# An RWKV-6 scan with a mixture of adapters on one core: last gates selected on logits and applied transposed, last tile in halves, first r and k apart, three output sums on GpSimd, a new order

## The chip, the cores and the metric

The kernel runs on 1 core of a Trainium2 chip. The metric is the device time of one execution in microseconds (us). The profile shows one execution by the hardware profiler; "span" is the part of it that the instructions cover. The engines are PE (TensorE matmul), PEld (TensorE weight load), DVE (VectorE), ACT (ScalarE), POOL (GpSimd) and SP (SyncE, which here only issues DMAs); "SPq" and "POOLq" are the instruction queues of SP and POOL.

## What is computed

Four batches of 768 steps, 8 heads of 48 channels. A recurrent attention with a decaying state, and behind it a top-2 mixture of eight rank-16 adapters:

```python
# per step t:   y[t] = r[t] . (state + (u*k[t]) x v[t]);   state = w[t]*state + k[t] x v[t]
x = y.transpose(0, 2, 1, 3).reshape(3072, 384)
logits = x @ w_gate                          # 8 experts
topk = two largest logits;  w = softmax over those two
out = x + sum over the two of  w_e * ((x @ A[e]) @ B[e])       # A: 384x16, B: 16x384
```

## The kernel before

The 3072 rows are 24 tiles of 128 steps; six consecutive tiles (a chunk row of one batch) share a running state. All 24 tiles are unrolled. Each step of each tile is a small Python function, called as `name.tile`; the list `ORDER` names all calls, and the scheduler is told to keep it (`manual_schedule` for all five engines). So every engine, SP with its DMAs included, executes its own instructions in the order in which they stand in that list, and an instruction that waits holds all that stand behind it on the same engine. The position of a call against calls of other engines has no effect by itself.

For tile t the steps are: `load_w`, `load_rk`, `load_v` (transfers, mostly two or four tiles at once); `ln` (ACT, log of w); `cs`, `ci` (PE, running sums of the logs) and `grow`, `exps` (ACT, exponentials); `mult` (DVE L362, r and k times these); `tr` (PE transposes) and `trev` (their copy); `amm` (PE, scores) and `aev` (DVE L453, masked scores); `rkp` and `dv` (POOL L379, L396), `dgmm` and `dgev` (the bonus term with u); `yi`, `ya` (PE, the tile's output); `kv` and `sev` (state and its copy); `xev` (DVE L529, the 128x384 result `xs`); `xk`, `xkev` (transpose of `xs` and its copy).

The adapters run in batches of tiles, `BATCHES = (4, 4, 4, 4, 4, 2, 1, 1)`, named after their last tile (3, 7, 11, 15, 19, 21, 22, 23): `lgmm` (PE logits), `gate` (ACT exp), `gmax` (DVE, the eight largest), `gsel` (DVE, those at or above the second), `gden` (DVE L579 sum of the two and L580 reciprocal), `gmul` (two POOL products, L599 and L600), `zmm` (PE, x @ A), `zw` (DVE L614, times the gates), `zT` (PE transpose) and `zTev` (its copy). Then per tile `dmm` (PE, @ B; where ACT makes the output an identity matmul adds `xs` first), `oev` (the 128x384 output `res`, on DVE L651, on ACT L649, or for tiles 22 and 23 on DVE L646 with the division) and `store` (SP L655, one DMA of 192 KB). `res` has 16 buffers; PSUM tiles of `y`, `xk`, `z`, `zT` and `d` share a ring of three.

SP issues the loads of w, of the first tiles and all stores. Its last entries in the old list, in order: the stores of tiles 2, 3, 1, 0, 6, 7, 4, 5, 11, 8, 9, 10, 14, 13, 12, 15, 17, 18, 19, 16, 20, 22, 21, 23, with loads between the first ones.

Of the kernel before, what the change touches and what calls it, by code (L numbers as in the profile page):

```python
# [8 lines left out]
F32 = mybir.dt.float32  # L9
# [42 lines left out]
SYNC = True  # L52
YA = False
COL = False
TAG = {('d', 22): 'y', ('d', 23): 'a_ps'}
ENGINES = {'out': {0: 'A', 3: 'A', 8: 'A', 12: 'A', 13: 'A', 15: 'A', 16: 'A', 18: 'A', 20: 'A', 21: 'A', 17: 'A'},
    'k_id16': {0: 'A'}, 'trev': {0: 'D', 5: 'D', 9: 'D'}, 'xkev': {-3: 'D', -2: 'D'}, 'sev': {0: 'D'}, 'dgev': {1:
    'D', 5: 'D'}, 'cast_v': {1: 'D'}, 'cast_b': {0: 'D'}, 'zTev': {3: 'A', 7: 'A', 11: 'A', 15: 'A', 19: 'A', 21: 'A',
    22: 'A', 23: 'A'}}
# [15 lines left out]
xkev.3 mult.7 amm.5 grow.8 dgev.5 aev.5 lgmm.2 trev.6 lgmm.3 gate.3 ci.8 gmax.3 gsel.3 load_rk.12 gden.3 zmm.3 exps.8
sev.4 load_v.12 ya.4 cs.9 tr.7 rkp.7 load_b.0 dv.4 xev.4 gmul.3 load_w.10 kv.6 ln.10 grow.9 trev.7 zw.3 dv.5 amm.6
ci.9 dgmm.6 yi.5 xk.4 zT.3 exps.9 sev.6 cast_b.0 xkev.4 mult.8 cs.10 rkp.8 aev.6 mult.9 zTev.3 kv.7 ya.5 dgmm.7
grow.10 sev.7 dgev.7 tr.8 dmm.2 ci.10 trev.8 ya.6 load_w.12 amm.7 kv.8 xev.5 xk.5 exps.10 cs.11 tr.9 sev.8 xkev.5 yi.7
oev.2 lgmm.4 aev.7 yi.8 grow.11 ln.12 dv.6 dv.7 xev.6 ci.11 dgmm.8 store.2 rkp.9 mult.10 kv.9 exps.11 xk.6 ya.7
# [10 lines left out]
grow.18 oev.6 gmax.11 amm.15 lgmm.12 trev.16 ci.18 dgev.15 dv.14 xk.13 exps.18 xkev.13 aev.15 yi.14 tr.17 ya.14 cs.19  # L90
store.3 yi.15 amm.16 zmm.11 sev.15 gsel.11 grow.19 trev.17 xev.14 ci.19 mult.18 xk.14 ln.20 tr.18 dgmm.16 ya.15
gden.11 load_w.22 exps.19 cs.20 xkev.14 dgmm.17 gmul.11 dv.15 dgev.17 yi.16 aev.16 load_rk.22 grow.20 trev.18 ya.16
mult.19 zw.11 kv.16 amm.17 store.1 zT.11 xev.15 ci.20 xk.15 dv.16 load_v.20 sev.16 exps.20 tr.19 cs.21 aev.17 rkp.19
zTev.11 xkev.15 grow.21 xev.16 dmm.8 dmm.11 amm.18 oev.8 mult.20 oev.11 lgmm.15 xk.16 yi.17 lgmm.13 lgmm.14 trev.19
gate.15 ci.21 dmm.9 ya.17 store.0 store.6 aev.18 gmax.15 kv.18 dv.17 xkev.16 xev.17 exps.21 amm.19 gsel.15 rkp.20
ln.22 ya.18 gden.15 oev.9 dgmm.19 dgmm.18 xk.17 store.7 store.4 store.5 dgev.19 sev.18 cs.22 gmul.15 xkev.17 dv.18
tr.20 grow.22 aev.19 zmm.15 yi.19 trev.20 lgmm.17 ci.22 ya.19 dv.19 rkp.21 exps.22 kv.19 xev.18 zw.15 sev.19 amm.20
store.11 store.8 zT.15 xev.19 cs.23 zTev.15 mult.21 dmm.10 store.9 dmm.13 rkp.22 oev.13 aev.20 xk.18 xkev.18 dgmm.20
tr.21 trev.21 xk.19 lgmm.16 mult.22 dmm.14 dgmm.21 oev.10 kv.20 xkev.19 rkp.23 dgev.21 amm.21 dmm.12 dv.20 lgmm.18
lgmm.19 yi.20 oev.14 grow.23 sev.20 gate.19 store.10 store.14 oev.12 aev.21 ya.20 dmm.15 ci.23 tr.22 exps.23 trev.22  # L100
gmax.19 yi.21 xev.20 gden.19 ya.21 xk.20 kv.21 dv.21 amm.22 mult.23 tr.23 store.13 store.12 oev.15 xkev.20 sev.21
gsel.19 zmm.19 gmul.19 trev.23 xev.21 store.15 dgmm.23 dgmm.22 xk.21 dgev.23 aev.22 xkev.21 amm.23 kv.22 sev.22 zw.19
zT.19 dv.22 yi.22 ya.22 dv.23 zTev.19 aev.23 xev.22 lgmm.20 lgmm.21 dmm.17 yi.23 ya.23 gate.21 gmax.21 oev.17 store.17
xk.22 xev.23 dmm.18 xkev.22 gsel.21 oev.18 dmm.19 zmm.21 gden.21 kv.23 lgmm.22 store.18 oev.19 store.19 xk.23 gmul.21
# [609 lines left out]
```

## Time and profile before

| | us |
|---|---|
| median of 3 runs (lowest, highest) | 86.1 (86.06, 86.43) |
| the profiled execution's own time | 85.72 |
| its span | 84.0 |
| PE, DVE, ACT, POOL busy | 76.6, 74.2, 68.9, 55.9 |
| DMA | 18.12 MB, mean 216 GB/s |

A windows view gives the busy time of each engine in a stretch of the span, then the granted TensorE clock (1.00 is full), the busy share of the 16 DMA engines, and GB/s moved. A row of groups gives line, engine, operation, tiles and shapes, the count, busy us and mean ns. A timeline row gives start, duration and the instruction, with the idle time before it and what ended it.

### The profile page before, as it was taken

What the parts mean: (1) busy time and instruction counts of PE and PEld (TensorE: products, weight loads), DVE (VectorE), ACT (ScalarE), POOL (GpSimd) and SP (SyncE); (2) the same over time, 40 slices, a digit from 0 to 9 for tenths busy, and PEclk for the clock granted to TensorE, in tenths of its full rate; (3) what the DMA queues carried; (4) which work ended last, traced back from release to release, by engine and by line L of the source; (5) the groups of instructions that cost most, each with busy time, mean ns of one, the idle gap of its engine ahead of it and who ended that gap; (6) DMA issues with size and microseconds to landing.
All of it is one profiled execution on the core that took longest, in us unless ns stands there. A gap on an engine that the chain in (4) does not pass through costs nothing.

```text
span 84.0 us, 3311 instructions
## 1 busy us (share of the span) xinstructions
PE 76.6 (91%) x1322; PEld 58.4 (69%) x1322; DVE 74.2 (88%) x157; ACT 68.9 (82%) x167; POOL 55.9 (67%) x89
## 2 busy tenths in 40 slices
PE   4897699999999999999999999999999999999710
PEld 1244276688887878788888688888779788887300
DVE  5019989999999999999999999999999999999740
ACT  6376679799999999999899989879898789866800
POOL 6306999689988667778999876379759483362000
PEclk9999999999999999999999999999999999999985
DMA  1899999999999999989999886988986026304681
GB/s 20 280 335 362 391 374 265 289 252 287 270 225 211 214 216 240 297 274 249 177 192 149 145 190 128 377 303 108 126 202 228 14 96 255 125 12 145 233 316 59
DMA packets 8943, 18.12 MB, mean 216 GB/s; under 512 B 992, under 2 KB 5216, under 8 KB 8928
## 3 DMA queue, kind: packets, MB, share of 16 engines
q1 hardware_dynamic: 6480, 11.82, 40.7%
q0 software_dynamic: 2448, 6.10, 40.3%
q8 instruction: 10, 0.16, 0.8%
q14 instruction: 5, 0.04, 0.2%
HBM read 19.29 MB, written 4.72 MB: 286 GB/s over the span
## 4 chain that ended last, share of the span: by engine, by line
PE 72%; DVE 15%; DMA 5%; issue 2%; SPq 1%; ACT 1%; ACTq 0%; DVEq 0%
PE trp L404 11%; PE xk_ps L538 9%; PE a_ps L442 8%; DVE rk L362 6%; PE y_ps L524 6%; PE s_ps L475 5%; DMA rk_first<-in_rk_dram 5%; PE d_ps L640 5%; PE z_ps L607 4%; PE y_ps L498 4%; PE cs_ps L351 4%; PE cs_ps L334 4%; PE cs_ps L333 3%; DVE at L453 3%; PE d_ps L639 2%; PE s_ps L559 2%
## 5 line engine op out<-in xcount | busy, mean ns | idle before, releaser
L453 DVE TENSOR_TENSOR at<-a_ps,strict 128x1024 f16<-128x1024 f32 x24 | 29.1, 1214 | 0.3
L379 POOL TENSOR_TENSOR rkp<-rk 128x384 f16<-128x384 f16 x20 | 18.2, 912 | 5.2 <-DVE rk L362 2.7
L396 POOL TENSOR_TENSOR dv<-v,dg 128x384 f32<-128x384 f16 x22 | 18.2, 835 | 3.7 <-ACT dg L200 3.0
L404 PE MATMUL trp<-ident,rk 128*128 128x128 bf16 x192 | 14.7, 219 | 0.5 <-DVE rk L362 0.5
L206 ACT COPY rkT<-trp 128x512 f32<-128x512 f32 x21 | 12.6, 600 | 1.2 <-PE trp L404 1.2
L404 PEld LDWEIGHTS <-rk 128*128 128x128 bf16 x192 | 11.7, 98 | 2.7 <-DVE rk L362 1.5
L346 ACT ACTIVATE e<-cs_ps 128x384 bf16<-128x384 f32 x24 | 12.0, 501 | 1.6 <-PE cs_ps L334 1.6
L529 DVE TENSOR_TENSOR xs<-dv,y_ps 128x384 f16<-128x384 f32 x24 | 13.1, 544 | 0.3 <-PE y_ps L524 0.2
L356 ACT ACTIVATE e<-cs_ps 128x384 bf16<-128x384 f32 x23 | 11.4, 497 | 1.8 <-PE cs_ps L351 1.7
L206 ACT COPY xkT<-xk_ps 128x384 f32<-128x384 f32 (+1 forms) x25 | 11.5, 462 | 0.4 <-PE xk_ps L538 0.2
L362 DVE TENSOR_TENSOR rk<-rk,e 128x768 bf16<-128x768 f16 x20 | 11.1, 560 | 0.0
L200 ACT CAST S_sb<-s_ps 128x384 bf16<-128x384 f32 x19 | 9.4, 492 | 0.7 <-PE s_ps L475 0.3
L442 PE MATMUL a_ps<-rkT 48*128 48x128 bf16 x192 | 9.5, 219 | 0.1
L324 ACT ACTIVATE logw<-w_in 128x768 f16<-128x768 f32 x11 | 9.3, 847 | 0.0
L334 PE MATMUL cs_ps<-logw,strict 128*128 128x384 f16 x24 | 8.2, 340 | 0.4 <-ACT logw L326 0.4
L538 PE MATMUL xk_ps<-ident,rkp 128*128 128x128 f16 x72 | 8.0, 219 | 0.4 <-POOL rkp L379 0.4
L351 PE MATMUL cs_ps<-logw,ident 128*128 128x384 f16 x24 | 8.0, 333 | 0.2 <-ACT e L346 0.2
L524 PE MATMUL y_ps<-v,at 128*128 128x48 f16 x176 | 8.0, 183 | 0.0
L538 PE MATMUL xk_ps<-ident,xs 128*128 128x128 f16 x72 | 8.0, 219 | 0.0
L524 PEld LDWEIGHTS <-at 128*128 128x128 f16 x192 | 7.3, 96 | 0.9
L362 DVE TENSOR_TENSOR rk<-rk_first,e 128x768 bf16<-128x768 f32 (+1 forms) x5 | 4.5, 913 | 3.7 <-DMA rk_first<-in_rk_dram 3.7
L640 PE MATMUL d_ps<-Ball,zT 128*128 128x384 f16 x24 | 7.5, 325 | 0.2 <-ACT zT L206 0.2
(76 smaller groups left out, 160.4 us busy)
## 6 DMA issues: line engine op xcount, KB each, us to landing
out_dram<-res SPq DMA_DIRECT2D x24, 192.0 KB, 2.6
w_in<-in_w_dram SPq DMA_DIRECT2D x11, 384.0 KB, 6.6
rk<-in_rk_dram POOLq DMA_DIRECT2D x10, 384.0 KB, 8.2
rk_first<-in_rk_dram SPq DMA_DIRECT2D x4, 384.0 KB, 6.0
v<-in_v_dram POOLq DMA_DIRECT2D x4, 384.0 KB, 8.5
v<-in_v_dram POOLq DMA_DIRECT2D x3, 192.0 KB, 10.6
w_in<-in_w_dram SPq DMA_DIRECT2D x2, 192.0 KB, 2.5
v_first<-in_v_dram SPq DMA_DIRECT2D x2, 192.0 KB, 7.1
```

Source lines behind the costliest of these rows:

```text
L206: nc.scalar.copy(out=out.bitcast(F32), in_=in_.bitcast(F32))
L346: nc.scalar.activation(out=e2[:, 0], in_=cs_ps[:, 0:HD], func=ACT.Exp, **(dict(bias=CENTRE) if CB else {}))
L362: return nc.vector.tensor_mul(rk2[:, lo:hi].rearrange("s m p h d -> s (m p h) d")[:, :, 0:D], st[t]["rk"][:, lo:hi].rearrange("s m (h d) - ...
L379: return nc.gpsimd.tensor_mul(p_, st[t]["rk"][:, 0], st[t]["rk"][:, 1])
L396: return nc.gpsimd.tensor_mul(dv_, st[t]["v16"], st[t]["dg"].rearrange("p (h o) -> p h o", o=1).to_broadcast([L, H, D]))
L404: nc.tensor.transpose(trp[:, m, p, :], rk2[:, m, p, :, :].rearrange("s a b -> s (a b)"), ident)
L442: nc.tensor.matmul(a_ps[:, g, p, :], lhsT=rkT[base:base + D, 1, p, :], rhs=rkT[base:base + D, 0, p, :], start=True, stop=True)
L453: nc.vector.tensor_mul(at, st[t]["a_ps"].rearrange("s g p f -> s (g p) f"), strict.to_broadcast([128, H, 128]))
L524: nc.tensor.matmul(d["y_ps"][:, h, :], lhsT=d["at"][:, g * P + p, :], rhs=d["v16"][:, h, :], start=(c == 0 and h == 0), stop=(h == H - 1), ...
L529: nc.vector.tensor_add(xs, st[t]["dv"].rearrange("p a b -> p (a b)"), st[t]["y_ps"].rearrange("p a b -> p (a b)"))
L538: nc.tensor.transpose(xk_ps[:, 3 * q + j, :], src[:, j * 128:(j + 1) * 128], ident16)
L640: nc.tensor.matmul(d_ps, lhsT=st[t]["zT"], rhs=Ball, start=not by_pe, stop=True)
```

## The change

- **First tile.** Its r and k come in two DMAs of 192 KB (`load_rr.0`, `load_kk.0`) instead of one of 384 KB.
- **Batches 22 and 23** (`TG`). The two largest are taken on the logits themselves; `gsel` writes a 128x128 mask, which `zT` transposes; `zmm` now makes two products, the logits repeated 16 times (weights `w16x`, made once by POOL in `m_wx`) and x @ A, both transposed; `zge` (ACT) is the exp of the first, `zw` (DVE) their product, and `zTev` (DVE) mask times product.
- **Tile 23 in halves.** `aev`, `ya`, `xev`, `oev` and `store` are split in two each.
- **Batches 3 to 21** (`GADD`). The sum of the two largest moves from DVE to POOL (`gadd`).
- **Output sums.** For tiles 4, 6 and 9 ACT copies the product and POOL adds `xs` (`oadd`); tiles 8, 12, 14 to 18 and 20 keep the sum on PE with ACT's copy. As before, ACT copies 11 outputs and DVE makes the rest.
- **Engines.** The casts of v (tile 1) and of B move from DVE to ACT; one identity cast, two small `dgev` and one `xkev` move from ACT to DVE.
- **Order.** `ORDER` is new throughout. On SP the stores now come in the order 0 (among the loads of w), 2, 7, 11, 5, 4, 19, 17, 16, 12, 1, 13, 15, 14, 6, 18, 10, 8, 20, 3, 21, 9, 22, and the two halves of 23. On DVE the outputs of tiles 22 and 23 come before the last steps of batches 15, 19 and 21.

```diff
+TG = (22, 23)
+GADD = (3, 7, 11, 15, 19, 21)
+RSPLIT = (0,)
...
-ENGINES = {'out': {0: 'A', 3: 'A', 8: 'A', 12: 'A', 13: 'A', 15: 'A', 16: 'A', 18: 'A', 20: 'A', 21: 'A', 17: 'A'},
...
+ENGINES = {'out': {4: 'G', 6: 'G', 8: 'A', 9: 'G', 12: 'A', 15: 'A', 14: 'A', 16: 'A', 17: 'A', 18: 'A', 20: 'A'},
+    'trev': {1: 'D', 3: 'D', 4: 'D'}, 'xkev': {-2: 'D', -3: 'D', 3: 'D'}, 'dgev': {1: 'D', 3: 'D', 5: 'D', 23: 'D'},
+    'sev': {6: 'D'}, 'zTev': {3: 'A', 7: 'A', 11: 'A', 15: 'A', 19: 'A', 21: 'A'}}
...
+xkev.18 dgmm.21 ya.19 xev.19 trev.21 kv.20 grow.23 amm.21 ci.23 dgev.21 rkp.22 tr.22 yi.20 ya.20 dv.20 xk.19 rkp.23
...
+oev.10 xkev.20 oadd.10 oadd.9 yi.22 dgmm.23 dgev.23 trev.23 ya.22 amm.23 dv.22 kv.22 sev.22 dmm.8 lgmm.13 lgmm.19
+lgmm.12 lgmm.14 yi.23 lgmm.15 oev.8 aeva.23 aevb.23 yaa.23 yab.23 xev.22 xk.22 gate.15 dv.23 xeva.23 xkev.22 lgmm.18
+lgmm.17 lgmm.16 xevb.23 kv.23 xk.23 xkev.23 lgmm.22 gmax.15 gmax.22 zmm.22 gsel.22 gsel.15 lgmm.23 gate.22 gden.22
+gmax.23 zge.22 zmm.23 zw.22 gsel.23 zT.22 zge.23 gate.23 zTev.22 zw.23 zT.23 gden.23 zTev.23 dmm.22 yi.21 lgmm.20
+dmm.23 zmm.15 oev.22 ya.21 oeva.23 gate.19 dv.21 gadd.15 gden.15 oevb.23 gmul.15 zw.15 zT.15 xev.21 gmax.19 zTev.15
+xk.21 dmm.15 oev.15 gsel.19 zmm.19 dmm.12 xkev.21 oev.12 dmm.14 lgmm.21 oadd.12 gadd.19 gden.19 oev.14 gmul.19 zw.19
+zT.19 dmm.13 zTev.19 oev.13 dmm.17 gate.21 gmax.21 oev.17 dmm.18 dmm.16 dmm.19 oev.19 oev.18 gadd.21 gden.21 gsel.21
+store.4 oadd.19 oadd.15 gmul.21 oadd.17 oev.16 oadd.16 oadd.13 oadd.14 zmm.21 zw.21 zT.21 zTev.21 store.19 oadd.18
+store.17 store.16 store.12 store.1 store.13 store.15 store.14 store.6 store.18 store.10 dmm.21 dmm.20 oev.21 oev.20
+oadd.8 oadd.20 store.8 store.20 store.3 oadd.21 store.21 store.9 store.22 storea.23 storeb.23
...
+    def load_half(t, m):
+        nc.sync.dma_start(out=st[t]["rk"][:, m], in_=flat(rk, t, 1, 2 * HD)[:, 0, m * HD:(m + 1) * HD])
...
+    def m_wx(t):
+        nc.gpsimd.tensor_copy(w16x, w16[:, :, ER:ER + E].rearrange("p j (e o) -> p j e o", o=1)
+                              .to_broadcast([128, 3, E, R]))
...
+    def aevh(t, lo):
...
+    def xevh(t, lo):
...
     def gate(t):
...
+        if t in TG:
+            ge = wk.tile([L, 1, 2], F32, name="ge2", bufs=2)
+            nc.scalar.activation(out=ge, in_=st[t]["top"][:, :, 0:2], func=ACT.Exp)
...
+    def gadd(t):
+        t0, n = gate_at[t]
+        st[t]["gsum"] = wk.tile([L, GMAX, 1], F32, name="gsum")[:, 0:n, :]
+        nc.gpsimd.tensor_add(st[t]["gsum"], st[t]["gtop"][:, :, 0:1], st[t]["gtop"][:, :, 1:2])
...
+            nc.vector.tensor_tensor(
+                out=st[t]["sel"], in0=lg_ps[:, t % NSLOT, :].rearrange("p (e o) -> p e o", o=1).to_broadcast([L, E, R]),
+                in1=st[t]["top"][:, :, 1:2].to_broadcast([L, E, R]), op=ALU.is_ge)
...
+    def zge(t):
+        st[t]["geT"] = wk.tile([ER, 128], F32, name="geT", bufs=2)
+        nc.scalar.activation(out=st[t]["geT"], in_=st[t]["z_ps"][:, 0, :], func=ACT.Exp)
...
+            for i in range(2):
+                for j in range(3):
+                    lhsT = w16x[:, j].rearrange("p e r -> p (e r)") if i == 0 else w16[:, j, 0:ER]
+                    nc.tensor.matmul(z_ps[:, i, :], lhsT=lhsT, rhs=st[t]["xT"][:, j, :], start=(j == 0), stop=(j == 2))
...
+            nc.vector.tensor_mul(st[t]["zg"], st[t]["z_ps"][:, 1, :], st[t]["geT"])
...
+            nc.vector.tensor_mul(zT_[:, 0, :], st[t]["zT_ps"][:, 0, :], st[t]["zg"])
...
+    def oadd(t):
+        if engine("out", t, "D") == "G":
+            return nc.gpsimd.tensor_add(st[t]["res"], st[t]["res"], st[t]["xs"])
...
+    def oevh(t, i):
+        c = slice(i * HD // 2, (i + 1) * HD // 2)
...
+        nc.vector.scalar_tensor_tensor(out=st[t]["res"][:, c], in0=st[t]["d_ps"][:, c], scalar=st[t]["den"],
+                                       in1=st[t]["xs"][:, c], op0=ALU.mult, op1=ALU.add)
...
+    def storea(t):
+        nc.sync.dma_start(out=out[t * 128:(t + 1) * 128, 0:HD // 2], in_=st[t]["res"][:, 0:HD // 2])
...
+    def storeb(t):
+        nc.sync.dma_start(out=out[t * 128:(t + 1) * 128, HD // 2:], in_=st[t]["res"][:, HD // 2:])
```

An `oadd` of a tile that is not on GpSimd issues nothing.

More of the change, by code (lines that the diff above doesn't have):

```diff
@@ L75 @@
[L75 to L79, printed above, removed]
@@ L90 @@
[L90 to L94, printed above, removed]
@@ L95 @@
[L95 to L104, printed above, removed]
@@ L416, in amm @@
         st[t]["a_ps"] = a_ps
+        if YA:
+            if t % NC:
+                st[t]["y_ps"] = pp.tile([L, H, D], F32, name="y_ps", **slot("y", t))
+            rows = [[(D, carried, t, p, 0) for p in range(P if t % NC else 0)] + [(128, score, t, p, 0) for p in range(P)],
+                    [(D, carried, t - 1, p, 1) for p in range(P if t and (t - 1) % NC else 0)]
+                    + [(128, score, t, p, 1) for p in range(P)]]
+            sent = [0, 0]
+            while rows[0] or rows[1]:
+                g = 0 if rows[0] and (not rows[1] or sent[0] <= sent[1]) else 1
+                n, fn, *args = rows[g].pop(0)
+                fn(*args)
+                sent[g] += n
+            return
         if t in PACK:
@@ L663 @@
                 before = done
-            elif f in ("rkp", "dv") and before is not None and SYNC:
+            elif f in ("rkp", "dv", "oadd", "zs") and None not in (done, before) and SYNC:
                 tc.add_manual_dep(done.ins, before.ins.name, mybir.DependencyInfo(
```

176 lines of the change are left out of this document (137 added, 39 removed).

## The prediction

> **What bounds the kernel now.** I read the page's engine table first, then a windows view cut at two points: the start of the first product on DVE (5.94) and the end of tile 19's output on DVE (76.95). The columns are PE, PEld, DVE, ACT, POOL busy, clock, DMA share, GB/s.
>
> ```profile
> span 84.0 us, 3311 instructions
> PE 76.6 (91%) x1322; PEld 58.4 (69%) x1322; DVE 74.2 (88%) x157; ACT 68.9 (82%) x167; POOL 55.9 (67%) x89
> 0.00:5.94 5.94, 4.27 (x12) 1.62 (x13) 1.24 (x3) 3.27 (x6) 2.02 (x12) 1.00 0.64 202
> 5.94:76.95 71.01, 69.67 (x1291) 55.36 (x1290) 69.70 (x142) 63.14 (x152) 53.87 (x77) 1.00 0.86 219
> 76.95:84.00 7.05, 2.65 (x24) 1.40 (x21) 3.26 (x13) 2.46 (x9) 0.00 (x0) 0.81 0.54 197
> ```
>
> Between 5.94 and 76.95 us DVE is busy 69.70 of 71.01 us and PE 69.67: both are full, and 1.31 us of DVE's time is idle. Nothing but less work on them makes this stretch shorter. What a change can save lies before it (DVE waits for the first r and k) and behind it (7.05 us, of which DVE computes 3.26). So I looked at the end next: the timeline there, and what SP waited for.
>
> ```profile
> 76.39 0.56 DVE L651 TENSOR_TENSOR res<-d_ps,xs 128x384 f32<-128x384 f32 x1
> 79.64 1.19 DVE L646 SCALAR_TENSOR_TENSOR res<-d_ps,den,xs 128x384 f32<-128x384 f32 x2 [0.23 <-PE d_ps L640]
> 78.03 3.15 SPq L655 DMA_DIRECT2D out_dram<-res  x5
> 80.85 0.33 SPq L655 DMA_DIRECT2D out_dram<-res  x1
> L655 SPq DMA_DIRECT2D out_dram<-res x24: 332/346/1034, 31.0 to 80.9; - x24
> SPq L655 <- DVE res L651: 31.8, 4, 19.5
> SPq L655 <- ACT res L649: 21.2, 5, 15.2
> ```
>
> The last row of `res` is done at 80.83 and the last store is issued at 80.85; five of 24 stores are issued from 78.03 on. The last two rows matter most for this change: SP stood still for 31.8 us in four waits, once for 19.5 us, until a DVE output came, and 21.2 us for ACT outputs. A store that waits holds the stores behind it. The DMA engines were not the limit there, but they are at the very end:
>
> ```profile
> 77.50:78.50 1.00, 0.73 (x12) 0.55 (x10) 0.83 (x6) 0.86 (x4) 0.00 (x0) 1.00 0.98 364
> 80.00:82.00 2.00, 0.17 (x1) 0.00 (x0) 0.82 (x2) 0.00 (x0) 0.00 (x0) 0.82 0.96 347
> 82.00:82.50 0.50, 0.00 (x0) 0.00 (x0) 0.00 (x0) 0.00 (x0) 0.00 (x0) 0.50 0.50 184
> 82.50:84.00 1.50, 0.00 (x0) 0.00 (x0) 0.00 (x0) 0.00 (x0) 0.00 (x0) 0.50 0.00 0
> ```
>
> With stores queued up, the 16 engines are busy 0.96 to 0.98 of the time and move 347 to 364 GB/s: that is their full rate. The data ends about half way through 82.00:82.50, at 82.25; the span ends 1.75 us later.
>
> **The change, part by part.**
>
> *The stores.* In the new list SP meets the store of tile 19 seventh of all stores. Behind it stand 17 tiles' worth: 17, 16, 12, 1, 13, 15, 14, 6, 18, 10, 8, 20, 3, 21, 9, 22 and the halves of 23. Many of these outputs will have been ready for 20 us and more, but by the rows of SP's waits they stay where they are until tile 19's output is there. From that moment, which I call T19, 18 x 196,608 bytes = 3.54 MB must leave. At 347 GB/s that is 10.2 us, at 364 it is 9.7. Issuing is no limit: 19 DMAs x 0.346 us = 6.6 us. Before, the same moment lay at 76.95, and only five stores were issued from 78.03 on, beside computing that went on until 80.83. I add 0.3 us for the wait and the issue ahead of the first byte (0.33 from the last store's row) and 1.75 behind the last: span = T19 + 0.3 + 10.2 + 1.75 = T19 + 12.25.
>
> The Trainium skill, "DMA: Bandwidth & Descriptors", section Bandwidth, lists 425 GB/s for one 16 MB load with the pair's other core idle, beside a limit of about 358 on HBM per core. By 425 the 3.54 MB would take an estimated 8.3 us, and the time would come out 1.9 us lower; the row here, 347 at a share of 0.96, stands with the page's lower number, and the trace decides.
>
> *When T19 comes.* Rows for DVE's work and the chain ahead of it, from the groups kept apart by shape (count | busy, mean ns):
>
> ```profile
> L202 DVE CAST v_first<-v_first 128x384 f16<-128x384 f32 x1 | 0.6, 610 | 0.0
> L202 DVE CAST Ball<-Ball_f 128x384 f16<-128x384 f32 x1 | 0.4, 360 | 0.0
> L579 DVE TENSOR_REDUCE den<-top 128x4 f32<-128x8 f32 x5 | 0.8, 152 | 0.0
> L202 DVE COPY dg<-s_ps 128x16 f32<-128x16 f32 x2 | 0.3, 170 | 0.0
> L208 DVE COPY rkT<-trp 128x1024 bf16<-128x1024 bf16 x3 | 2.0, 661 | 0.0
> L208 DVE COPY xkT<-xk_ps 128x384 f16<-128x384 f16 x2 | 0.7, 351 | 0.3 <-PE xk_ps L538 0.3
> L614 DVE TENSOR_TENSOR zw<-z_ps,g 128x128 f16<-128x128 f32 x2 | 0.6, 292 | 0.2
> L614 DVE TENSOR_TENSOR zw<-z_ps,g 128x256 f16<-128x256 f32 x1 | 0.4, 411 | 0.0
> L589 DVE SCALAR_TENSOR_TENSOR g<-ge,top 128x8 f32<-128x8 f32 x2 | 0.5, 226 | 0.1
> L580 DVE RECIPROCAL den<-den 128x2 f32<-128x2 f32 x1 | 0.2, 166 | 0.0
> L592 DVE TENSOR_TENSOR g<-ge,top 128x16 f32<-128x16 f32 x1 | 0.2, 167 | 0.0
> L651 DVE TENSOR_TENSOR res<-d_ps,xs 128x384 f32<-128x384 f32 x11 | 5.9, 548 | 0.0
> L599 POOL TENSOR_TENSOR g<-g,ge 128x32 f32<-128x32 f32 x5 | 1.3, 251 | 3.2 <-ACT res L649 1.4 <-DVE den L579 1.0 <-DVE g L592 0.7
> L600 POOL TENSOR_TENSOR g<-g,den 128x32 f32<-128x32 f32 x5 | 1.2, 239 | 1.3 <-DVE den L580 1.0
> L206 ACT COPY zT<-zT_ps 128x256 f32<-128x256 f32 x5 | 1.9, 379 | 0.3 <-PE zT_ps L624 0.2
> L649 ACT COPY res<-d_ps 128x384 f32<-128x384 f32 x11 | 5.3, 480 | 0.9 <-PE d_ps L640 0.6
> L640 PE MATMUL d_ps<-Ball,zT 128*128 128x384 f16 x24 | 7.5, 325 | 0.2 <-ACT zT L206 0.2
> ```
>
> First what DVE does. Gone: the casts of v and B (0.61 + 0.36) and six sums of two (6 x 0.15 = 0.9), together 1.87. Added: two `dgev` (2 x 0.17 = 0.34); one `xkev` of 768 columns, between the rows for 384 and 1024 columns, 0.54; two `zTev` as products of 128x128 (2 x 0.29 = 0.58; no such step with an f16 PSUM input is in the trace, its bounds are 0.17, the smallest step, and 0.41); two masks at 0.29 instead of 0.23 (0.13); three steps cut in halves, each an extra fixed part, which from 292 ns at 128 columns and 411 at 256 is 0.17 (0.5). Together 2.09. So DVE gains nothing: +0.2. The identity cast falls into DVE's early wait.
>
> Then what is left behind tile 19's output: one reciprocal, one comparison, one 128x256 product and one output, 0.17 + 0.17 + 0.41 + 0.55 = 1.3 us. Before it was 3.26. The new order puts tiles 22 and 23 ahead and thereby 2.0 us of DVE's work in front of T19. DVE's work from the first product to T19 is 69.70 + 2.0 + 0.2 = 71.9 us.
>
> *The head.* These rows show what the first product waits for.
>
> ```profile
> 1.71 0.42 SPq L261 DMA_DIRECT2D rk_first<-in_rk_dram  x1
> 4.39 0.49 ACT L346 ACTIVATE e<-cs_ps 128x384 bf16<-128x384 f32 x1 [0.38 <-PE cs_ps L334]
> 5.94 0.56 DVE L362 TENSOR_TENSOR rk<-rk_first,e 128x384 bf16<-128x384 f32 x1 [3.66 <-DMA rk_first<-in_rk_dram]
> ```
>
> r and k come as one DMA that ends DVE's wait at 5.94; the exponential for r is done at 4.88. With r alone, half the bytes, the wait ends between 4.88 and 5.94; I take 5.3, a gain of 0.6 us (bounds 0 and 1.06). k comes when it came before, and the transposes, which need both, gain the less.
>
> *Stalls of the new tail.* In the new list, batch 19 is the last large one, with little beside it. DVE's `zw.19` stands right behind its reciprocal and waits for the two POOL products, 0.25 + 0.24 = 0.5 us. The next DVE step, output 13, needs a matmul that PE has behind the transposes of `zw.19`: about 0.3 + 0.3 = 0.6 us. Output 19 then needs the copy of `zT.19` (0.38), the matmul for 17, ACT's output 17 (0.48, which frees the PSUM slot in the ring of three) and its own matmul (0.33 twice): 1.5 us with 0.9 of other work in it, 0.6 us. Sum 1.7; between 0.5 (most of it overlaps) and 3.5 (each hand-over costs twice as much). The 1.3 us of idle in the middle stay.
>
> T19 = 5.3 + 71.9 + 1.3 + 1.7 = 80.2 us. Its floor, with r free at 4.88 and no idle at all, is 76.8.
>
> *Edits at nothing.* POOL's three sums (its rows are under 1 us each for this size) and `m_wx` lie on an engine that is busy 67% of the time; without that cover they would push `dv` and `xev` and so DVE, up to 3 us. PE loses three identity matmuls and gains six of 128 columns, which is about even. The transposed gates shorten the chain of tiles 22 and 23; but nothing waits for these tiles any more, since their stores are the last of a queue of 10 us. The halves of tile 23 are worth nothing for the same reason.
>
> **Sum.** Span 80.2 + 12.25 = 92.45 us. The profiled execution before took 85.72 for a span of 84.0, 1.72 more: 94.2 us against its 85.72. The median of the three runs, 86.1, is 0.38 higher than the profiled one, so 94.2 may be 0.4 low.
>
> **The rivals.**
>
> *The burst is limited by issue, not data.* Then 19 x 0.35 = 6.6 us in place of 10.2, and the time is 90.6. For it: only 2 to 2.3 us of queued stores are to be seen before, never ten. Against it: the share of 0.96 in those 2 us. 0.06.
>
> *The middle gets worse.* The order is new for all 24 tiles, and PSUM's ring of three or POOL's queue may hold PE and DVE where they are now full; 1.31 us of idle could easily be 4. Each us moves T19 by as much: about 97 us, and more. For it: POOL has three more sums, `m_wx` and six `gadd`, in order with `dv`. Against it: POOL has 28 us of idle. 0.09.
>
> *Not slower: the stores leave as they get ready.* If a ready store is not held by one that waits, on SP or behind it, the burst disappears. Then the end is tile 20's output, which comes T19 + 0.17 + 0.5 + 0.41 + transposes, copy and two matmuls (1.5) + 0.48 = T19 + 3.1, and 3.17 us more as now (80.83 to 84.0). At T19 = 80.2 that gives 88.2, still slower; it is even from T19 = 77.7 down, 0.9 above the floor. Against it: SP's waits of 31.8 and 21.2 us. 0.03, of which 0.02 faster by more than 0.5% and 0.01 within it.
>
> **How the numbers follow.** My forecast, the burst behind tile 19 at the DMA engines' full rate, has 0.82. Its own bounds: T19 at 76.8 to 82, and 9.7 or 10.2 us, give 90.3 to 96. The range 90.5 to 97 holds this, the first rival and a part of the second. A measurement here can tell 0.5% from no change (86.06 to 86.43 is 0.4%). All but the third rival is slower: 0.97.
>
> **What would show it.** Right: in the profile after, SP's waits show one of over 15 us for an L798 output, and then some 19 stores issued without a gap, at 340 to 365 GB/s and a DMA share above 0.9, for about 10 us, while PE and DVE are idle for the last 8 us or so; the slices of the DMA row are near 0 just ahead of it. DVE's busy time is 74 to 75 us, and output 19 lies at 77 to 82. The chain that ended last ends in DMAs. Wrong: stores of tiles 12, 1 or 6 before output 19; a burst well above 365 GB/s; output 19 before 76.8; or a DVE row far under 72 us.

## The result, and the profile after

| | before | after |
|---|---|---|
| median of 4 runs (lowest, highest), us | 86.08 (85.99, 86.43) | 107.91 (105.96, 109.06) |
| profiled execution, us | 85.72 | 108.71 |
| its span | 84.0 | 106.6 |

The changed kernel is slower: ratio 1.237, 95% interval 1.224 to 1.249. The forecast was 94.2, with 97.0 as its upper end, so the time is outside the range. Executions of the changed kernel and of its variants scatter by several us, so every ratio below compares undisturbed executions with those of the kernel before on the same chip, while the medians are over all.

The page of the profile after: the engine table, and of the 40 slices the clock row and the two DMA rows.

```profile
span 106.6 us, 3330 instructions
PE 82.9 (78%) x1325; PEld 61.2 (57%) x1325; DVE 74.8 (70%) x158; ACT 69.4 (65%) x165; POOL 59.7 (56%) x99
PEclk9999999999999997555899999999999999999655
GB/s 71 246 374 404 340 284 283 269 256 219 212 212 99 208 137 209 332 371 20 16 177 108 66 162 0 6 104 119 152 6 0 0 9 3 0 69 367 367 366 160
```

DVE is busy for 74.8 us, as forecast (74 to 75), so the work is not what grew. Two places stand out. The last slices move 366 and 367 GB/s with almost nothing ahead of them: the forecast's burst. And the clock row falls to 5 in the middle, where before it had none below 9 ahead of the tail. That was not forecast.

A windows view, cut at the first product (5.59), around the hole (the stretch near 38 to 46 us in which nearly nothing runs), at the end of tile 19's output (94.54) and 10.3 us later (columns as before: PE, PEld, DVE, ACT, POOL, clock, DMA share, GB/s):

```profile
5.59:38.00 32.41, 30.96 (x499) 22.54 (x498) 28.83 (x51) 26.38 (x59) 25.50 (x36) 1.00 1.03 259
38.00:46.00 8.00, 0.40 (x5) 0.21 (x3) 0.19 (x1) 1.45 (x4) 0.20 (x1) 0.71 0.91 244
46.00:52.00 6.00, 6.00 (x68) 4.67 (x67) 4.38 (x10) 4.36 (x11) 4.43 (x7) 0.54 0.35 137
52.00:94.54 42.54, 40.57 (x748) 31.93 (x745) 38.80 (x91) 33.74 (x87) 27.11 (x43) 1.00 0.30 58
94.54:104.85 10.31, 0.95 (x5) 0.33 (x5) 1.12 (x4) 0.74 (x2) 0.44 (x2) 0.73 0.94 334
104.85:106.60 1.75, 0.00 (x0) 0.00 (x0) 0.00 (x0) 0.00 (x0) 0.00 (x0) 0.50 0.19 58
```

From 38 to 46 us the engines hardly compute (PE 0.40 us, DVE 0.19, ACT 1.45), while the DMA engines are busy 0.91 of the time: everyone waits for a transfer. From 46 to 52 PE is busy throughout, but at a granted clock of 0.54 with 68 matmuls (before, 10 us held some 200), and DVE gets only 4.38 us of work in 6. The fifth row is the burst; in the sixth the last data still land (a share of 0.19 over the row), and then nothing moves.

*The end.* The timeline at the end, and SP's own waits:

```profile
93.98 0.56 DVE L798 TENSOR_TENSOR res<-d_ps,xs 128x384 f32<-128x384 f32 x1 [0.83 <-PE d_ps L787]
94.57 8.38 SPq L825 DMA_DIRECT2D out_dram<-res  x17
103.00 0.48 SPq L819 DMA_DIRECT2D out_dram<-res  x1
103.52 0.49 SPq L822 DMA_DIRECT2D out_dram<-res  x1
SPq L825 <- DVE res L798: 56.0, 3, 26.3
SPq L825 <- DVE g L720: 19.0, 1, 19.0
```

L798 is an output made on DVE, L825 the store of a tile, L819 and L822 are the stores of tile 23's halves. Tile 19's output ends at 94.54; 30 ns later 17 stores start to be issued without a gap, and the two halves follow. SP stood for a DVE output (L798) three times, at most 26.3 us. From 94.54 to the end of the span it is 12.06 us; the forecast said 12.25.

*The hole.* The timeline around 38 us (SP, and the first instructions behind the hole), and the waits that end it:

```profile
37.27 0.55 DVE L798 TENSOR_TENSOR res<-d_ps,xs 128x384 f32<-128x384 f32 x1
37.84 0.34 SPq L825 DMA_DIRECT2D out_dram<-res  x1
38.23 3.94 SPq L267 DMA_DIRECT2D w_in<-in_w_dram  x5
44.55 0.84 ACT L350 ACTIVATE logw<-w_in 128x768 f16<-128x768 f32 x1 [7.68 <-DMA w_in<-in_w_dram]
45.81 0.56 DVE L388 TENSOR_TENSOR rk<-rk,e 128x768 bf16<-128x768 f16 x1 [7.99 <-ACT e L382]
45.83 0.48 PE L359 MATMUL cs_ps<-logw,rest 128*128 128x384 f16 x1 [7.60 <-ACT dg L212]
```

Read it from the bottom: PE and DVE waited 7.6 and 8.0 us, both behind ACT; ACT waited 7.68 us for a load of w, and went on at 44.55. SP issued that load, with four others, from 38.23 on, right behind the store at 37.84. That store is tile 0's, and it waited for output 0 (37.27 to 37.82). So a store held five loads. The list says why ACT waited so long: `store.0 ... load_w.22 ln.22 exps.12 ... load_w.14`. ACT takes the log of tile 22, ten tiles ahead of its use, in front of the exponential of tile 12, and all that stands behind it on ACT waits for a load that has just been issued.

### The profile page after: what moved, and what is told of

Same layout as the page of the kernel before. It is cut to its first block, busy times and chain, and to the rows that moved or that the text cites. A ratio compares the mean times of both kernels' runs of the same rounds, so it can differ in the third digit from the quotient of the medians.

```text
span 106.6 us, 3330 instructions
## 1 busy us (share of the span) xinstructions
PE 82.9 (78%) x1325; PEld 61.2 (57%) x1325; DVE 74.8 (70%) x158; ACT 69.4 (65%) x165; POOL 59.7 (56%) x99
## 4 chain that ended last, share of the span: by engine, by line
PE 64%; DVE 9%; DMA 6%; ACT 5%; issue 4%; POOL 2%; SPq 0%; POOLq 0%; DVEq 0%; ACTq 0%
PE trp L430 10%; PE xk_ps L639 8%; PE a_ps L493 7%; DMA w_in<-in_w_dram 6%; PE warm_ps L252 5%; PE cs_ps L377 4%; PE y_ps L623 4%; PE s_ps L569 4%; PE cs_ps L359 4%; PE cs_ps L360 4%; PE d_ps L787 3%; PE z_ps L747 3%; PE y_ps L597 3%; DVE zw L758 2%; PE s_ps L668 1%
## 5 line engine op out<-in xcount | busy, mean ns | idle before, releaser
L508 DVE TENSOR_TENSOR at<-a_ps,strict 128x1024 f16<-128x1024 f32 x23 | 27.9, 1215 | 2.4 <-PE a_ps L493 2.4
L388 DVE TENSOR_TENSOR rk<-rk,e 128x768 bf16<-128x768 f16 x20 | 11.5, 586 | 8.0 <-ACT e L382 8.0
L430 PE MATMUL trp<-ident,rk 128*128 128x128 bf16 x192 | 15.6, 227 | 0.3 <-ACT rkT L218 0.2
L430 PEld LDWEIGHTS <-rk 128*128 128x128 bf16 x192 | 12.4, 102 | 1.5 <-DVE rk L388 0.6
L629 DVE TENSOR_TENSOR xs<-dv,y_ps 128x384 f16<-128x384 f32 x23 | 12.5, 543 | 1.1 <-PE y_ps L623 1.1
L359 PE MATMUL cs_ps<-logw,rest 128*128 128x384 f16 x20 | 7.2, 358 | 7.7 <-ACT dg L212 7.6
L218 ACT COPY xkT<-xk_ps 128x384 f32<-128x384 f32 (+1 forms) x24 | 10.9, 458 | 1.6 <-PE xk_ps L639 1.5
L798 DVE TENSOR_TENSOR res<-d_ps,xs 128x384 f32<-128x384 f32 x11 | 6.0, 554 | 3.9 <-PE d_ps L787 3.8
L787 PE MATMUL d_ps<-Ball,zT 128*128 128x384 f16 x24 | 8.0, 343 | 0.5 <-ACT zT L218 0.4
L405 POOL TENSOR_TENSOR rkp<-rk_first 128x384 f16<-128x384 f32 x4 | 4.3, 1094 | 6.4 <-DMA rk_first<-in_rk_dram 3.7
```

What stands on the lines that cost most here:

```text
L218: nc.scalar.copy(out=out.bitcast(F32), in_=in_.bitcast(F32))
L388: return nc.vector.tensor_mul(rk2[:, lo:hi].rearrange("s m p h d -> s (m p h) d")[:, :, 0:D], st[t]["rk"][:, lo:hi].rearrange("s m (h d) - ...
L405: return nc.gpsimd.tensor_mul(p_, st[t]["rk"][:, 0], st[t]["rk"][:, 1])
L430: nc.tensor.transpose(trp[:, m, p, :], rk2[:, m, p, :, :].rearrange("s a b -> s (a b)"), ident)
L508: nc.vector.tensor_mul(at, st[t]["a_ps"].rearrange("s g p f -> s (g p) f"), strict.to_broadcast([128, H, 128]))
L629: nc.vector.tensor_add(xs, st[t]["dv"].rearrange("p a b -> p (a b)"), st[t]["y_ps"].rearrange("p a b -> p (a b)"))
```

## Experiments

Two theories. **Forecast, mended:** the burst costs what was forecast, and the hole (store 0 ahead of the loads) makes up what is missing. **Rival:** the burst is a symptom; the new order is slow by itself, and the parts (gates, POOL's sums, split loads) would be faster in the old order. Each variant has line numbers of its own.

### The hole and the burst, each undone

**Loads ahead of store 0**: the changed kernel with one entry moved.

```diff
-... oev.0 oadd.0 store.0 dgmm.9 ... load_w.22 ln.22 ... load_w.18 load_w.20 ...
+... oev.0 oadd.0 dgmm.9 ... load_w.22 ln.22 ... load_w.18 load_w.20 store.0 ...
```

> The changed kernel with one entry of SP's list moved: the store of tile 0 stands behind the five loads of w instead of ahead of them. Load theory (ACT's log of tile 22 waits 7.7 us for a load that SP holds behind that store, and PE then runs at half clock for some 6 us): the stall of 7.7 us and about 3 us of slow PE go, tile 19's output comes at 84 instead of 94.5 us, the burst of stores behind it stays at 12 us: time 97 to 99. Rival, the new order itself holds the engines: less than 2 us gained, 105 or more. Rival, the loads collide with others when they are issued early: the stall goes but the first 20 us get longer by some us, 100 to 103.

Measured: 97.33 (96.73 to 98.47), ratio 1.131 (1.125 to 1.138). The hole is gone, and with it some 9 us by the ratios (1.237 to 1.131) and 10.6 between the medians; in the two traces output 19 ends 11.5 us earlier. The timeline and windows of this run let the forecast's terms be read one by one:

```profile
82.44 0.56 DVE L798 TENSOR_TENSOR res<-d_ps,xs 128x384 f32<-128x384 f32 x1 [0.82 <-PE d_ps L787]
83.02 8.38 SPq L825 DMA_DIRECT2D out_dram<-res  x17
5.72:20.00 14.28, 12.23 (x178) 8.06 (x177) 12.86 (x20) 11.62 (x25) 12.44 (x17) 1.00 1.05 316
20.00:72.20 52.20, 51.85 (x1021) 42.40 (x1020) 51.08 (x94) 48.67 (x118) 42.73 (x62) 1.00 0.73 174
72.20:83.00 10.80, 9.03 (x111) 6.15 (x111) 8.01 (x38) 5.21 (x17) 2.06 (x8) 1.00 0.01 3
```

DVE's work from the first product to output 19 is 12.86 + 51.08 + 8.01 = 71.95 us. Its idle time is 1.42 + 1.12 in the first two rows and 2.79 in the tail.

**Stores in the order in which outputs get ready**, with store 0 still ahead of the loads.

```diff
-store.4 oadd.19 ... store.19 oadd.18 store.17 store.16 store.12 store.1 store.13 ... storea.23 storeb.23
+... load_w.20 store.2 store.3 store.1 ... oev.7 store.7 ... oev.12 store.12 ... oev.19 store.19 ... oev.20 store.20
```

> The changed kernel with its stores in the order in which the outputs get ready; the store of tile 0 stays ahead of the loads of w. Burst theory: the computing is unchanged (stall included), the end lies some 3.2 us behind the last output (97.8 in the profile after) instead of 12 us behind tile 19's: 5.5 to 6 us gained, 101 to 103. Rival, the last stores are hidden or something else sets the end: under 2 us gained.

Measured: 102.53 (99.32 to 103.53), against 107.91: 5.4 us less, and within the expected 101 to 103; the runs scatter by 4 us, so the size is rough. In the trace the last output ends at 97.96 (97.78 in the changed kernel), and the span 3.1 us later in place of 8.8. ACT's wait for w is still there (8.0 us).

**Both.**

> The changed kernel with both moves on SP: loads of w ahead of the store of tile 0, and stores in the order of readiness. If load and burst theory hold and add up: the last output at 87 to 88 us, the span 90 to 91.5, the time 91.5 to 93.5, so the remaining 5 to 7 us over the kernel before are the head and the tail of the new order. Rival, the rest of the order is as good as before: 86 to 87.

Measured: 91.32 (90.44 to 96.16), ratio 1.063 (1.056 to 1.071); 91.5 to 93.5 was expected. From the first experiment to this one the burst's part is 6.0 us. Run once more on another chip, beside the late loads below:

> The changed kernel with both repairs of the stores once more, for a ratio beside the variants with ordinary gates (1.077) and with the denominators on DVE (1.079): theory, both of these parts are gains of one to two per cent in the order made for them, and this kernel is at 1.056 to 1.071 again: 90.6 to 91.9. Rival: the three cannot be told apart, 1.072 to 1.082: 92 to 92.8.

Measured: 91.88 (91.57 to 93.35), ratio 1.070 (1.068 to 1.073), so 5 to 6 us remain after both repairs. In the trace of the first of these two runs (91.32), output 19, the last output and the window behind it are

```profile
81.83 0.56 DVE L798 TENSOR_TENSOR res<-d_ps,xs 128x384 f32<-128x384 f32 x1 [0.83 <-PE d_ps L787]
85.10 0.48 ACT L796 COPY res<-d_ps 128x384 f32<-128x384 f32 x1 [0.75 <-PE d_ps L787]
85.58:88.70 3.12, 0.00 (x0) 0.00 (x0) 0.00 (x0) 0.00 (x0) 0.00 (x0) 0.54 0.36 129
```

The last output ends at 85.58, 3.19 us behind output 19 (82.39), and the span 3.12 us later.

**The early log moved back, store 0 left where it is.**

```diff
-... load_w.22 ln.22 exps.12 ... load_w.14 ... load_w.20 ... cs.22 ...
+... exps.12 ... load_w.14 ... load_w.20 load_w.22 ... ln.22 cs.22 ...
```

> The changed kernel with the log of tile 22 moved on ACT to its place ahead of tile 22's sums, and its load of w behind the other four; the store of tile 0 stays ahead of these loads. It tells which wait the stall is. If the early log alone holds ACT: the whole stall goes, 97 to 99. If the late issue of the loads is enough by itself (tile 14's w then arrives at about 45 us and is needed at about 39): 4 to 6 us of stall stay, 103 to 106.

Measured: 106.97 (105.90 to 109.33), ratio 1.234 (1.227 to 1.242) where the changed kernel has 1.237; more than either theory said. ACT now waits 5.51 us (tile 14's log) in place of 7.68, and the time hardly moves. So the early log is not the cause; the late loads are.

### The hole and the burst, each made alone in the old order

**The kernel before with the changed kernel's list of late stores**, nothing else.

```diff
-... store.1 ... store.6 ... store.16 store.20 ... store.23
+... store.19 store.17 store.16 store.12 store.1 store.13 ... store.3 store.21 store.9 store.22 store.23
```

> The kernel before with only the late part of its list of stores replaced by that of the changed kernel: seventeen tiles' stores behind that of tile 19; nothing else differs. By the forecast's formula the span is T19 + 12.25, with T19 = 76.95 as in the kernel before: span 89.2, time 90.9. With the 12.06 us that the changed kernel showed, 90.7. Range 90 to 92. Rival (ready stores are not really held, or the burst needs the changed kernel's slow middle): 86 to 87.

Measured: 90.97 (90.85 to 91.04), ratio 1.059 (1.055 to 1.064); forecast by the formula 90.9. In its timeline and windows:

```profile
76.31 0.56 DVE L650 TENSOR_TENSOR res<-d_ps,xs 128x384 f32<-128x384 f32 x1
76.90 8.91 SPq L654 DMA_DIRECT2D out_dram<-res  x18
77.20:87.20 10.00, 2.32 (x21) 1.18 (x18) 2.94 (x13) 2.18 (x8) 0.00 (x0) 0.70 0.95 346
```

Output 19 ends at 76.87 and the span (89.0) 12.13 us later. The price of the burst is shown apart from all else in the change.

**The kernel before with its five last loads of w behind store 0.**

```diff
-... load_w.14 ... oev.0 ... load_w.16 ... load_w.18 ... load_w.20 ... load_w.22 ... store.0 ...
+... oev.0 store.0 load_w.14 load_w.16 load_w.18 load_w.20 load_w.22 ...
```

> The kernel before with one thing moved on SP: the store of tile 0 and behind it the five loads of w for tiles 14 to 22, which there were issued from 31.4 us on, now stand together, so that the loads are issued behind output 0 (ready at 36.5). ACT's log of tile 14 ran at 36.82. Theory: a load behind a waiting store is late by as much, the log waits until the first of the five has landed, all engines behind it run dry and PE comes back at half rate: a wait of 2 to 6 us and one to three us more for PE, 89 to 95. Rival: the log and the tiles behind it have slack, or the loads land at once: 85.8 to 87.

Measured: 92.63 (92.21 to 92.77), ratio 1.080 (1.078 to 1.083).

```profile
42.16 0.84 ACT L323 ACTIVATE logw<-w_in 128x768 f16<-128x768 f32 x1 [5.19 <-DMA w_in<-in_w_dram]
43.52 0.48 PE L332 MATMUL cs_ps<-logw,rest 128*128 128x384 f16 x1 [4.73 <-ACT e L355]
42.00:48.00 6.00, 4.48 (x49) 3.53 (x50) 3.64 (x11) 4.54 (x11) 3.51 (x6) 0.50 1.06 281
```

A wait of 5.19 us costs 6.9 us in time: behind it PE runs at half clock (0.50), and DVE does 3.64 us of work in 6. The hole, too, needs nothing else of the change.

**The kernel before with each store behind its output** (the reverse of the burst).

> The kernel before with only its list of stores changed: each store but that of tile 2 stands right behind the step that makes its output (and behind the last load of w). If the held stores of the kernel before cost something at its end, it is the backlog there: the data of the last store ended at 82.25 us, 1.4 us behind the last output, where one store alone takes 0.3 + 0.57 us; so about 0.4 us less, 85.3 to 85.6 against 85.8. Rival: the backlog only moves, or stores now collide with the loads in the middle (DMA share 0.86 there): 85.8 to 86.8.

Measured: 86.82 (86.12 to 89.97), ratio 1.009 (1.005 to 1.012): the rival holds. The stores that the old list held back cost it nothing.

### The parts alone in the old order

**r and k of tile 0 apart** (`RSPLIT = (0,)`, two DMAs).

> The kernel before with one part of the change alone: r and k of the first tile in two DMAs, the old order otherwise. In the runs with the new order the first product began at 5.7 us instead of 5.94 and the second ended at 6.8 instead of 6.97. Head theory (the first transfer bounds the start): 0.2 us gained, 85.8, hardly told from no change; the 0.6 us of the prediction would give 85.4. Rival, one more DMA on SP delays the later loads: 86.2 to 86.5.

Measured: ratio 1.002 (0.999 to 1.005). No gain.

**Gates of 22 and 23 on logits, tile 23's output in halves** (`TG = (22, 23)`, `zge`, `m_wx`, `oeva`, `oevb` put into the old list).

> The kernel before, in its old order, with the transposed gates for tiles 22 and 23, and the output and store of tile 23 in halves. There tile 23's chain sets the end. Theory: the chain loses an exponential (0.24 us) and a product (0.36 us) and the last store is half as long (0.3 us): 0.5 to 0.9 us gained, 85.1 to 85.5. Rival, the second product of zmm and the additional copy on DVE take as much as they save: 85.8 to 86.3.

Measured: 87.96, ratio 1.025 (1.022 to 1.029): a miss, slower by 2.2 us, more than the rival allowed. The end of its timeline:

```profile
79.97 0.29 DVE L753 TENSOR_TENSOR zg<-z_ps,geT 128x128 f32<-128x128 f32 x1 [0.43 <-ACT geT L730]
81.60 0.50 PE L785 MATMUL d_ps<-Ball,zT 128*128 128x384 f16 x1 [0.91 <-DVE zT L774]
82.14 0.74 DVE L807 SCALAR_TENSOR_TENSOR res<-d_ps,den,xs 128x192 f32<-128x192 f32 x2 [0.60 <-PE d_ps L785]
```

DVE's product waits for ACT's exponential of the repeated logits, tile 23's product with the mask (81.26) stands behind tile 22's output (80.73 to 81.35) on DVE, and the last matmul took 0.50 us (0.34 before). The last output ends at 82.88 instead of 80.83. Where I put the new steps may have a part in this; no other place was tried.

**POOL's sums**: first all of them (`GADD`, and outputs 4, 6, 9 as `oadd`), then the denominators alone.

> The kernel before, in its old order, with the sums of two on POOL and the new assignment of the outputs (three sums on POOL, PE's identity matmul for eight instead of eleven). DVE's work falls by 0.9 us, PE's by 0.5. Theory, both are full in the middle, so it counts: 0.3 to 0.9 us gained. Rival, POOL's additional 4 us delay the bonus products and the gates: 0 to 1.5 us lost.

> The kernel before with only the six sums of the gates' denominators moved from DVE to POOL (each right behind DVE's maxima), outputs as before. Theory: POOL works in order and now waits for DVE's maxima, which holds the dv and rkp products behind it; that was the greater part of the 6.9 us which this edit and POOL's three output sums lost together: 89.5 to 92. Rival: the output sums and the changed places of the output copies lost it, and this edit alone is worth between -0.5 and +1: 85.3 to 86.8.

Measured: all 93.74, ratio 1.080 (1.072 to 1.088), a miss; the denominators alone 90.51, ratio 1.048 (1.039 to 1.056). Of the second, two waits in the timeline, a window of 20 us beside the same one of the kernel before, and what follows on PE:

```profile
25.92 0.21 POOL L691 TENSOR_TENSOR gsum<-top 128x4 f32<-128x4 f32 x1 [3.03 <-DVE top L685]
28.93 0.56 DVE L627 TENSOR_TENSOR xs<-dv,y_ps 128x384 f16<-128x384 f32 x1 [2.60 <-POOL dv L420]
20.00:40.00 20.00, 18.11 (x331) 14.55 (x329) 16.23 (x32) 16.29 (x39) 12.90 (x20) 0.91 0.92 221
20.00:40.00 20.00, 20.00 (x394) 16.48 (x391) 19.57 (x44) 19.34 (x48) 16.02 (x25) 1.00 1.03 246
29.55 0.50 PE L637 MATMUL xk_ps<-ident,xs 128*128 128x128 f16 x3 [1.90 <-DVE xs L627]
29.55:32.55 3.00, 3.00 (x36) 2.23 (x37) 3.00 (x6) 1.53 (x4) 1.57 (x2) 0.50 0.93 179
```

A sum of 0.21 us stood on POOL for 3.03 us waiting for DVE's maxima, and held what stands behind it: two DMA issues, an `rkp` and the `dv` product. DVE then waited 2.60 us for `dv`, and PE 1.90 us for DVE. Behind that pause PE ran 3 us at a granted clock of 0.50 (last two rows). DVE does 16.23 us of work in 20 (third row) where it did 19.57 (fourth, before). The sums stood right behind the maxima; no other place was tried in the old order. Between the two runs the output sums, together with the new assignment of the outputs, account for the rest, some 3 us; these two were not run apart.

**All three in the old order.**

> All three parts together in the old order (SP's list with the old order of stores and loads). Theory, the new order alone is what cost 22 us and the parts are harmless: 84.3 to 86. Rival, the parts themselves carry the 5 us that were left when the two SP faults were repaired: 88 to 91.

Measured: 95.46, ratio 1.106 (1.099 to 1.112), above both expectations. The rival theory (faster parts under a slow order) falls: in the old order the three cost together what they cost one by one (0.2, 2.5 and 8.0 per cent). The moves of casts and copies between engines, and the halves of `aev`, `ya` and `xev`, were not run alone.

### What remains after both repairs

**The kernel before with batches 19 and 21 behind tiles 22 and 23.**

```diff
-... zw.19 zT.19 ... gate.21 ... zT.21 ... gate.22 ... oev.22 oev.21 ... oev.23 store.23
+... gate.22 ... oev.22 ... gate.19 gmax.19 gden.19 dmm.23 oev.23 ... zw.19 zT.19 ... gate.21 ... oev.21 store.21
```

> The kernel before with one thing moved: the gates and outputs of batches 19 and 21 (tiles 16 to 21) stand behind those of tiles 22 and 23, as in the changed kernel; stores follow their outputs. Theory: what is left of the loss after both repairs (4.7 to 5.2 us) is this order of the tail, because a batch behind the last full work of PE and DVE runs hand-over by hand-over: 2.5 to 6 us more than 85.9: 88.4 to 92. Rival: the tail's order is free and the rest of the loss lies in the middle or in POOL's new work: 85.8 to 87.

Measured: 93.95 (93.59 to 95.35), ratio 1.096 (1.088 to 1.104): more than expected. Its windows:

```profile
60.00:70.00 10.00, 10.00 (x201) 8.23 (x198) 9.90 (x22) 8.41 (x21) 7.59 (x11) 1.00 0.50 124
70.00:80.00 10.00, 7.88 (x133) 5.50 (x131) 7.16 (x20) 5.11 (x17) 1.84 (x3) 0.86 0.22 81
80.00:89.00 9.00, 6.18 (x34) 3.18 (x32) 3.55 (x16) 2.94 (x8) 0.93 (x4) 0.58 0.36 131
```

Up to 70 us it is the kernel before (DVE 9.90 of 10); the loss lies in the tail, where DVE works 3.55 us in 9 and the granted clock falls to 0.58. The engines wait for one another there: POOL once 6.69 us for DVE, ACT 4.08 for PE, DVE 1.25 for ACT.

**Three variants of the repaired kernel**: ordinary gates for 22 and 23; denominators on DVE; batch 15 and the first steps of 19 ahead of 22 and 23.

> The changed kernel with both repairs of the stores, and tiles 22 and 23 with the ordinary gates of the kernel before (values, not logits; product with z on the plain side; copy of the transposed result on ACT), at the same places of the list. Theory: the transposed gates are worth nothing here, since these two tiles come four to ten us ahead of the end and nothing waits for them: 90.8 to 91.8, as with them (91.3). Rival: they shorten the stretch in which DVE has only these two tiles to work on, or lengthen it as in the old order (2.2 us): 92 to 93.5, or 89 to 90.5.

> The changed kernel with both repairs of the stores, and the six sums of denominators back on DVE (one reduction of 0.15 us each) in place of POOL. Theory: in the tail each of the last three batches loses a way from DVE to POOL and back, about 0.4 us each, and no product on POOL waits any more for DVE's maxima in the middle; 0.4 to 1.5 us less than 91.3: 89.8 to 90.9. Rival: in the order that was made for them the sums cost nothing, and DVE gets 0.9 us more to do: 91.3 to 92.2.

> The changed kernel with both repairs of the stores (loads ahead of the first store, stores in the order in which outputs get ready), and in its tail the gate steps of batch 15, and the first ones of batch 19, put ahead of the chain of tiles 22 and 23; tiles 22 and 23 still have the transposed gates. Theory: what is left against the kernel before (91.3 against 86.1) is the tail, where batches 15, 19 and 21 run one behind the other with 0.6 to 1.1 us of waiting at each hand-over and nothing beside them; with batch 15 gone from it, 1 to 2.5 us less: 88.8 to 90.3. Rival: the tail is limited by the hand-overs through the ring of three PSUM slots whatever the order of the batches: 90.8 to 92.5.

Measured: 93.44 (ratio 1.077, 1.070 to 1.084), 93.60 (1.079, 1.073 to 1.086) and 95.99 (1.093, 1.086 to 1.100), against 1.070 (1.068 to 1.073) for the repaired kernel; all three lie above the times that their theories gave. The first cannot be told from it; the second is at best even. So in the order made for them neither part costs what it does in the old one, and neither is what remains. The third made it worse. It shows only that the tail is sensitive to its order, not which order is good.

No version tried beats the kernel before.

## Why the prediction was right and wrong

The terms of its sum, with what the kernel without the hole and the changed kernel showed:

| term | forecast | loads ahead | after |
|---|---|---|---|
| first product | 5.3 | 5.72 | 5.59 |
| DVE's work to output 19 | 71.9 | 71.95 | 72.20 |
| idle in the middle | 1.3 | 2.54 | 13.96 |
| stalls of the new tail | 1.7 | 2.79 | 2.79 |
| output 19 ends | 80.2 | 83.0 | 94.54 |
| from there to the end of the span | 12.25 | 12.0 | 12.06 |
| around the span | 1.72 | 2.2 | 2.1 |

The column "after" is worked out from the windows shown: DVE's work is 28.83 + 0.19 + 4.38 + 38.80; of the 88.95 us between 5.59 and 94.54 the rest, 16.75, is idle. The tail's part is read from one more window of the changed kernel, DVE 8.05 us in 10.84, so 2.79:

```profile
83.70:94.54 10.84, 9.03 (x111) 6.15 (x111) 8.05 (x39) 5.21 (x17) 2.11 (x8) 1.00 0.01 3
```

**Right: the burst.** A wait of over 15 us for an L798 output (26.3), 19 stores without a gap, 334 to 367 GB/s at a share of 0.94, 12.06 us behind output 19. It came out in three kernels, one of them the old order, within 0.3 us. Of the two figures of the Trainium skill that the prediction weighed ("DMA: Bandwidth & Descriptors", section Bandwidth: 425 GB/s, and a limit of about 358), these stores of 192 KB kept near the lower: 334 to 367 GB/s over 10 us.

**Right: DVE's work**, to 0.1 us where the hole is gone, with all its small edits.

**Wrong: "the 1.3 us of idle in the middle stay".** This step failed: 13.96 us of idle in place of 1.3, so 12.7 of the 14.5 us that the profiled execution lies above the forecast. The prediction walked through what a held store does to the stores behind it, and gave no word to the loads behind it on the same queue. The new place of store 0, among the loads of w, stands in the account of the change ahead of it. Without this stall the kernel runs in 97.3, just above the range; the middle still has 2.54 us of idle there, 1.2 more than forecast, and why is open. The stall has two parts: ACT's 7.68 us, and what PE loses at half clock behind it. The Trainium skill, "TensorE: Matmul & The Clock Gate", Part 1, says that an idle gap of more than about 3.4 us takes PE back to half clock. Behind gaps of 7.60 and 4.73 us the rows here agree: the granted clock averages 0.54 and 0.50 over windows of 6 us. They also show that a shorter gap can do it: behind the 1.90 us in the run with the denominators on POOL it was 0.50 for 3 us.

**Mis-sized: the stalls of the new tail**, 1.7 forecast, 2.79 measured, within its bounds (0.5 to 3.5). Its working priced three waits of DVE at 0.5, 0.6 and 0.6 us. In the changed kernel they took 0.79, 0.66 and 0.83, and the first was for PE's product x @ A, not for POOL.

**Mis-sized: the head.** The first product began 0.22 to 0.35 us earlier, not 0.64, and alone in the old order the split gains nothing (1.002). In the trace of that run the first product begins 0.31 us earlier (5.63), but the product for tile 1 at 8.79 us, where it began at 8.77 before.

**"Edits at nothing".** POOL's sums did lie beside other work in the new order, but its cover was the order: in the old one they cost 4 us (denominators) and 7 us (all), past the "up to 3 us" named for the loss of it. A part of that is PE at half clock, which the prediction did not price. The shorter chain claimed for the transposed gates is not shown by any run: alone they made it 2.2 us longer.

**The rivals.** Issue as the limit: no, the DMA engines were busy 0.94 of 10.31 us. But the 19 issues took 9.4 us (8.38 + 0.48 + 0.49), not 6.6, so the margin was smaller than the prediction had it. The middle getting worse: it did, but by SP's queue and not by PSUM's ring or POOL, and at 12.7 us more than the 1.3 of before, where the rival spoke of 4 us of idle in all. Stores that leave as they get ready: no in the change. With that made true, its working fits: output 19 + 3.1 + 3.17 was said, 82.39 + 3.19 + 3.12 measured. It is still slower than before: output 19 came at 82.39, and by the rival it would have had to come at 77.7 to be even. The old order moved in one point, batches 19 and 21 behind 22 and 23 (with stores behind their outputs), shows that this alone can cost 8 us.

What is left in the repaired kernel (91.32) is idle time of DVE. The first pair of rows runs from the first product to the last output, the second over the last 10.83 us of it; the repaired kernel comes first in each.

```profile
5.71:85.58 79.87, 73.69 (x1313) 56.65 (x1311) 72.92 (x154) 65.97 (x160) 57.62 (x87) 1.00 0.77 210
5.94:80.83 74.89, 72.32 (x1312) 56.76 (x1310) 72.96 (x154) 65.60 (x161) 53.87 (x77) 1.00 0.85 219
74.75:85.58 10.83, 7.36 (x77) 4.42 (x73) 6.25 (x22) 4.57 (x13) 1.57 (x7) 1.00 0.52 183
70.00:80.83 10.83, 9.60 (x161) 7.21 (x158) 9.99 (x31) 7.81 (x23) 2.62 (x7) 1.00 0.48 174
78.95 0.69 DVE L758 TENSOR_TENSOR zw<-z_ps,g 128x512 f16<-128x512 f32 x1 [0.79 <-PE z_ps L747]
80.30 0.56 DVE L798 TENSOR_TENSOR res<-d_ps,xs 128x384 f32<-128x384 f32 x1 [0.65 <-PE d_ps L787]
83.22 0.42 DVE L758 TENSOR_TENSOR zw<-z_ps,g 128x256 f16<-128x256 f32 x1 [0.69 <-POOL g L728]
84.77 0.56 DVE L798 TENSOR_TENSOR res<-d_ps,xs 128x384 f32<-128x384 f32 x1 [1.13 <-PE d_ps L787]
```

DVE's work is the same (72.92 and 72.96 us), and its idle time 6.95 us in place of 1.93. Of the 5.0 us between them 3.7 lie in the last 10.83 us. Five waits make most of that: the four shown here and the 0.83 us ahead of output 19. Open is which of these hand-overs would have to go to bring the repaired kernel from 91.3 to 86; the one reordering tried made it worse.

## What to carry to other kernels

When a waiting DMA moves on an in-order queue, list all that stands behind it, loads first: a late store cost its bytes at the end, a late load stopped every engine here and then cost the clock. Read a burst as (bytes behind the last waiting store) / (rate seen in the trace when stores queue up) from the moment that store is released; that held to 0.3 us in three kernels. An operation that is free beside other work in one order may hold a full engine in another: price a small operation on an in-order engine by how long it will wait, and by what waits behind it.

## What was not expected of the hardware

- A pause of 4.7 us on PE cost 6.9 us in time, one of 7.6 us 9 to 11: behind each, the granted clock averaged 0.50 to 0.54 over 6 us. A pause of 1.90 us was followed by 3 us at 0.50.
- Stores moved at 334 to 367 GB/s in every burst, while loads early in the changed kernel reached 404.
- Early in an execution the granted clock reads 1.00 while matmuls take up to 1.7 times as long. In the changed kernel's profile eight transposes took 1.06 us at 9.64, in the one before 0.61 us at 7.05:

```profile
9.64 1.06 PE L430 MATMUL trp<-ident,rk 128*128 128x128 bf16 x8
7.05 0.61 PE L404 MATMUL trp<-ident,rk 128*128 128x128 bf16 x8
```
